# A transformer block on one core: LayerNorm's normalization moved to VectorE, and smaller changes of order, buffers and engines around it

## The chip, the cores and the metric

The kernel runs on one core of one Trainium2 chip. The time is device time in microseconds (us) of that core, as a median over executions. A ratio below is the mean time of one kernel's fast runs over that of the other's fast runs of the same rounds, on the same chip, so it is not quite the ratio of the medians that are quoted. "Faster" means faster by over 2% with a 95% interval.

Engines: TensorE (PE; PEld is its weight load), VectorE (DVE), ScalarE (ACT), GpSimd (POOL), and SyncE, which issues the DMAs.

## The reference

One pre-LayerNorm transformer block in bf16, with S = 2048 tokens, D = 1024, 32 heads of 32, and F = 3584:

```python
x = A_x
h = x + _A_ref(_layernorm(x, axis=-1), A_wqkv, A_wo)      # softmax(q k^T / sqrt(32)) v, then @ wo
h2 = h + _B_ref(_layernorm(h, axis=-1), B_w1, B_b1, B_w2, B_b2)   # gelu_tanh(. @ w1 + b1) @ w2 + b2
```

The exponentials of the softmax are the large fixed cost: 32 heads x 2048 x 2048. The kernel makes them on ScalarE in 1024 instructions of 128 x 1024 elements, which it calls `PT<-ps`: 967.2 us of busy time in the kernel before.

## The kernel before

The kernel builds a graph of tasks. A list scheduler with a cost model then fixes the order of each engine's instructions, and semaphores follow from the dependencies.

The stages, named by what ScalarE does:

- **Lead-in.** For each of four blocks of 512 tokens: LayerNorm, transposes, K and V (and, for the first block, Q) of head group 0, and then 8 exponentials for that block's keys: 32 in all. A head group is 4 heads; there are 8.
- **Middle.** Attention of four chunks of 512 queries. A chunk is 256 exponentials, 32 for each head group. In between, TensorE does background work on one PSUM bank: in chunk 0 the projections of the other groups (`rest_of_projections`), in chunks 1 to 3 the Q projections that were put off ("late Q"), and the output projection, LN2 and FFN of the chunk before.
- **Tail.** Output projection, LN2 and FFN of the last chunk, on eight PSUM banks, with no attention left.

LayerNorm: VectorE makes the statistics, GpSimd makes 1/sqrt with two `pow`, and one of the two subtracts and multiplies:

```python
def layer_norm(tiles, prio, norm="dve"):
    ...                                   # bn_stats, bn_aggr on VectorE; add, pow, pow on GpSimd
    for k, (x_ap, B_x, o_ap, B_o) in enumerate(tiles):
        eng, cost = (dve, 0.58) if norm == "dve" else (pool, 1.4)
        eng(lambda e, ...: e.tensor_scalar(o_ap, x_ap, mvr[...], rden[...], ALU.subtract, ALU.mult), cost, ...)

def x_slot(tt):                           # a ring of six tiles of x
    s = tt % 6
    ...
```

The lead-in and the projections after it:

```python
for tc in range(4):
    tts = list(range(4 * tc, 4 * tc + 4))
    ev = "act" if tc == 0 else "dve"      # who copies transposes out of PSUM
    for h in ((0, 1), (2, 3)) if tc == 0 else ((0, 1, 2, 3),):
        ln_tiles([tts[k] for k in h], 0, "dve" if tc == 0 else "pool")
        for k in h:
            tr_tile(tts[k], lb(), ev)
    ...
    proj(1, 0, tc, lb(), ev)              # K
    if tc == 0:
        proj(0, 0, 0, lb(), ev, direct=True)   # Q
    for k in range(8):
        att.qk(0, [(k % 2, 4 * tc + k // 2)])  # one unit: QK for one exponential
        ...                               # V after k == 1 and k == 3
        lead_pv(4)

def rest_of_projections():
    for g in range(1, G):
        for tc in range(4):
            proj(1, g, tc, 7, "dve")      # K, four token blocks
        proj(0, g, 0, 7, "dve")           # Q: to DRAM and back by DMA
        if g < 7:
            ...                           # V for a later group, four pieces
    for g in range(G):
        proj(0, g, 1, 7, "dve")           # Q of chunk 1, all groups
```

The end of a head group's attention, and the last stages:

```python
def finish(self, qc, g, pr, bank):
    dve(... Dsb <- ps ...); dve(... Osb <- ps ...)      # denominators, numerators
    if pr == 1:
        for k in range(4):
            dve(... v.reciprocal(Dsb[:, 128k:128k+128]) ..., 0.93)
        dve(... OT[:, g, :] = Osb * Dsb ...)            # one OT for all chunks

def wo_ln2(R, qc, banks):
    for j in range(2):                    # column half outer, row block inner
        for t4 in range(4):
            for k, g in enumerate([7, 0, 1, 2, 3, 4, 5, 6]):
                mm(bank, OT[:, g, t4 * P:(t4 + 1) * P], R.w1[:, s:s + 2, g, :], k == 0, k == 7, ...)
            ...
    for t4 in range(4):
        layer_norm(...); transposes(..., "dve", 0)

# ffn1: bias add, square, inner polynomial and product on VectorE, tanh on ScalarE
dve(... v.tensor_scalar(R.xh[:, i, :], psum[:, bank, :], b1f[:, fc:fc + 1], None, ALU.add) ...)

for qc in range(1, NCH):                  # the middle
    if qc + 1 < NCH:
        late_q(R1, qc + 1)
    wo_ln2(R1, qc - 1, [7])
    ffn1(R1, qc - 1, [7]); ffn2(R1, qc - 1, [7])
    attention_chunk(qc)
```

The softmax here doesn't subtract the row's maximum and nothing guards it: scores larger than these inputs give would overflow.

## Time and profile before

| | before |
|---|---|
| median of 3 runs | 1263.97 us (1263.61 to 1265.93) |
| span of the profiled run | 1261.5 us |
| lead-in, to the start of the 33rd exponential | 130.3 us |
| middle, to the end of the last exponential | 986.5 us |
| tail | 144.7 us |

The three stages are read from ScalarE's timeline: 1024 exponentials stand in it, so the 33rd start and the last end cut the span.

First the page of the kernel before: busy time by engine with its share of the span, then the busy tenths in 40 slices (PEclk is the clock granted to TensorE), then the chain of work that ended last, as shares of the span by engine. In what follows L638 is the exponential, L498 the normalization, L435 and L439 matmuls of projections and FFN, L649 and L653 the PV matmuls, L629 QK.

```profile
span 1261.5 us, 37733 instructions
PE 1154.2 (91%) x17266; PEld 465.2 (37%) x17276; DVE 686.6 (54%) x1186; ACT 1027.8 (81%) x1145; POOL 83.6 (7%) x108
...
ACT  3322899999999999999989999999999999940210
POOL 4760000000002000000010000000100000001000
PEclk8668999999899999999999999999999999978989
...
PE 57%; ACT 27%; DVE 10%; POOL 4%; issue 2%; DMA 0%; POOLq 0%; DVEq 0%
```

TensorE is busy for 91% of the span and ScalarE for 81%, so the average names no culprit. The slices do: ScalarE is nearly idle in the first four, where GpSimd has most of its work and the clock granted to TensorE sags, and again in the last five.

The groups of instructions, with shapes kept apart (count, busy us, mean ns of one; then the idle time before them and what ended it):

```profile
L638 ACT ACTIVATE PT<-ps 128x1024 bf16<-128x1024 f32 x1024 | 967.2, 1037 | 87.8 <-PE ps L629 79.6 <-PE ps L653 3.7
...
L498 POOL TENSOR_SCALAR xb<-xrb,mvr,rden 128x1024 bf16<-128x1024 bf16 x8 | 30.2, 3782 | 0.4 <-POOL rden L494 0.2 <-DVE st L483 0.2
...
L498 DVE TENSOR_SCALAR xb<-xrb,mvr,rden 128x1024 bf16<-128x1024 bf16 x2 | 1.0, 544 | 1.8 <-POOL rden L494 1.8
```

GpSimd needs 3782 ns for a 128 x 1024 tile that VectorE normalizes in 544 ns. Of ScalarE's 87.8 us of waiting before exponentials, nearly all is for QK (L629).

GpSimd's timeline in the lead-in (start, duration, engine, line, operation, count):

```profile
25.46 7.56 POOL L498 TENSOR_SCALAR xb<-xrb,mvr,rden 128x1024 bf16<-128x1024 bf16 x2 [0.19 <-POOL rden L494]
...
50.21 15.07 POOL L498 TENSOR_SCALAR xb<-xrb,mvr,rden 128x1024 bf16<-128x1024 bf16 x4 [0.18 <-DVE st L483]
...
73.91 7.55 POOL L498 TENSOR_SCALAR xb<-xra,mvr,rden 128x1024 bf16<-128x1024 bf16 x2
```

Three blocks of four tiles, 15.1 us each, start about 24 us apart (the first and the third are split into two rows of two tiles). So 15.1 us of a block's 24 are normalization on GpSimd. ScalarE's timeline at the end of the lead-in:

```profile
95.52 7.69 ACT L638 ACTIVATE PT<-ps 128x1024 bf16<-128x1024 f32 x8 [8.28 <-PE ps L629]
130.34 1.94 ACT L638 ACTIVATE PT<-ps 128x1024 bf16<-128x1024 f32 x2 [27.14 <-PE ps L629]
```

After 8 exponentials in 7.69 us, ScalarE waits 27.14 us for the first QK of head group 1. In that time TensorE makes that group's K (four blocks), Q and four V pieces.

The busy time of each engine by stage:

```profile
core 0: us, PE busy (x) PEld busy (x) DVE busy (x) ACT busy (x) POOL busy (x), PEclk, DMA share, GB/s
...
25.50:130.30 104.80, 74.33 (x1194) 37.26 (x1192) 41.55 (x87) 31.58 (x33) 50.13 (x20) 0.77 0.41 104
130.30:343.50 213.20, 208.31 (x3896) 92.71 (x3900) 105.19 (x213) 210.43 (x225) 0.00 (x0) 0.98 0.16 50
343.50:1116.80 773.30, 730.06 (x11396) 270.17 (x11388) 432.05 (x686) 761.10 (x853) 18.99 (x48) 0.99 0.32 94
...
1150.00:1206.30 56.30, 51.24 (x223) 22.62 (x226) 51.29 (x90) 13.24 (x21) 0.00 (x0) 0.95 0.33 93
```

In the lead-in no engine is near its limit, and the granted clock is 0.77. In the rest TensorE has 208.3 of 213.2 us in chunk 0 and ScalarE 210.4: both are nearly full. VectorE is nearly full (51.3 of 56.3 us) in the last row, which is the tail's FFN1; TensorE has as much (51.2), but its timeline shows that it is the one that waits:

```profile
1123.16 15.69 PE L439 MATMUL ps<-a_w1r,OT 128*128 128x512 bf16 x64 [5.69 <-issue]
...
1201.53 0.39 PE L439 MATMUL ps<-b2t,two_row 128*128 128x512 bf16 x1 [0.82 <-DVE b_xh L728]
1204.87 0.39 PE L439 MATMUL ps<-b2t,two_row 128*128 128x512 bf16 x1 [2.94 <-DVE b_xh L728]
1206.32 0.61 PE L439 MATMUL ps<-b2t,two_row 128*128 128x512 bf16 x1 [1.07 <-DVE b_xh L728]
1206.72 3.62 PE L439 MATMUL ps<-a_w2r,gT 128*128 128x512 bf16 x8
```

The output projection starts 6.4 us after the last exponential (1116.8). At the border to FFN2, TensorE waits for VectorE's bias adds (b_xh, L728), which hand back PSUM banks: the last FFN1 matmul ends at 1200.3, and the first FFN2 matmul with weights starts only at 1206.72. After that wait the granted clock is 0.50 (1206.7 to 1210.3): 8 matmuls take 3.62 us.

### The profile page before, as it was taken

To read this page: it belongs to the slowest core of one execution; us is meant where nothing else is said; L and a number is where in the kernel's file an instruction comes from. 1 tells how busy PE (TensorE), PEld (TensorE's weight loads), DVE (VectorE), ACT (ScalarE), POOL (GpSimd) and SP (SyncE) were. 2 spreads that over 40 slices of the span, in tenths; PEclk is the share of its full clock that TensorE was granted. 3 is DMA by queue.
4 is the path that set the end of the run, shared out by engine and by line. 5 is a ranking of instruction groups with operands and counts; after the bars stand their busy time and mean duration, and the time that the engine had idled before them with its cause. 6 is when DMAs were issued, how large, how long until landed. Compare 5 with 4: busy or idle time off the path is not lost.

```text
span 1261.5 us, 37733 instructions
## 1 busy us (share of the span) xinstructions
PE 1154.2 (91%) x17266; PEld 465.2 (37%) x17276; DVE 686.6 (54%) x1186; ACT 1027.8 (81%) x1145; POOL 83.6 (7%) x108
## 2 busy tenths in 40 slices
PE   6677999999999999999989999998899999977988
PEld 3333444443333333333333333332333333323434
DVE  5335355555347888223367884323688822337971
ACT  3322899999999999999989999999999999940210
POOL 4760000000002000000010000000100000001000
PEclk8668999999899999999999999999999999978989
DMA  5190020003333323144332331423333304402404
GB/s 134 53 250 30 15 82 15 15 17 121 101 105 90 94 85 111 35 123 144 112 104 61 93 94 35 135 65 117 98 110 103 101 18 124 130 17 59 117 12 139
DMA packets 163137, 109.26 MB, mean 87 GB/s; under 512 B 25377, under 2 KB 160417, under 8 KB 162466
## 3 DMA queue, kind: packets, MB, share of 16 engines
q1 hardware_dynamic: 162978, 106.85, 29.2%
q8 instruction: 135, 2.21, 0.7%
q14 instruction: 24, 0.20, 0.1%
HBM read 96.22 MB, written 10.35 MB: 84 GB/s over the span
## 4 chain that ended last, share of the span: by engine, by line
PE 57%; ACT 27%; DVE 10%; POOL 4%; issue 2%; DMA 0%; POOLq 0%; DVEq 0%
PE ps L435 30%; ACT PT L638 26%; PE ps L439 9%; PE ps L649 9%; PE ps L629 8%; POOL xb L498 4%; DVE a_xh L728 3%; DVE gT L736 1%; DVE stg L544 1%; DVE Dsb L667 1%; DVE a_uu L732 1%; PE ps L504 1%; DVE Osb L663 1%; DVE st L483 1%; DVE Dsb L661 1%
## 5 line engine op out<-in xcount | busy, mean ns | idle before, releaser
L638 ACT ACTIVATE PT<-ps 128x1024 bf16<-128x1024 f32 x1024 | 967.2, 1037 | 87.8 <-PE ps L629 79.6
L649 PE MATMUL ps<-PT,V 128*32 128x512 bf16 x2048 | 322.0, 392 | 8.3 <-DVE Osb L663 4.3
L653 PE MATMUL ps<-PT,ones_50 128*32 128x512 bf16 x2048 | 322.1, 392 | 0.0
L629 PE MATMUL ps<-QT_65,KT_63 32*128 32x512 bf16 x2048 | 211.1, 390 | 17.7 <-ACT PT L638 17.2
L435 PE MATMUL ps<-hnT,a_w1r 128*32 128x512 bf16 x3200 | 211.2, 382 | 14.9 <-DVE a_xh L728 13.9
L435 PE MATMUL ps<-a_w2r,gT 128*32 128x512 bf16 x2688 | 196.5, 381 | 0.0
L649 PEld LDWEIGHTS ps<-PT,V 128*32 128x32 bf16 x2048 | 96.8, 97 | 125.3 <-issue 36.0
L629 PEld LDWEIGHTS ps<-QT_65,KT_63 32*128 32x128 bf16 x2048 | 53.1, 91 | 222.4 <-ACT PT L638 173.5
L661 DVE COPY Dsb<-ps 64x512 f32<-64x512 f32 x64 | 44.4, 694 | 131.1 <-PE ps L653 129.8
L435 PE MATMUL ps<-xnT,Wall 128*32 128x512 bf16 x1536 | 107.4, 400 | 8.3 <-DVE stg L544 6.1
L435 PEld LDWEIGHTS ps<-hnT,a_w1r 128*32 128x32 bf16 x3200 | 72.6, 96 | 114.4 <-issue 38.5
L667 DVE RECIPROCAL Dsb<-Dsb 128x128 f32<-128x128 f32 x128 | 114.2, 926 | 1.0
L435 PEld LDWEIGHTS ps<-a_w2r,gT 128*32 128x32 bf16 x2688 | 68.5, 96 | 81.9 <-issue 28.3
L653 PEld LDWEIGHTS ps<-PT,ones_50 128*32 128x32 bf16 x2048 | 96.8, 97 | 0.0
L734 ACT ACTIVATE b_th<-b_uu 128x512 f32<-128x512 bf16 x28 | 17.6, 630 | 84.2 <-DVE b_uu L732 84.2
L728 DVE TENSOR_SCALAR a_xh<-ps,b1f 128x512 bf16<-128x512 f32 x84 | 63.0, 750 | 36.2 <-PE ps L435 34.4
L488 POOL CAST mvb<-mv 128x2 bf16<-128x2 f32 (+2 forms) x21 | 4.5, 218 | 1057.6 <-DVE mv L485 1057.6
L435 PE MATMUL ps<-Wall,xnT 128*32 128x256 bf16 x2048 | 67.3, 274 | 3.3 <-DVE V L602 2.4
L758 DVE SCALAR_TENSOR_TENSOR a_ost<-ps,hch 128x512 bf16<-128x512 f32 x24 | 16.4, 684 | 97.0 <-PE ps L435 96.9
L544 DVE CAST stg<-ps 128x512 bf16<-128x512 f32 x46 | 31.2, 678 | 55.7 <-PE ps L435 55.6
L435 PEld LDWEIGHTS ps<-xnT,Wall 128*32 128x32 bf16 x1536 | 37.4, 100 | 61.7 <-issue 20.6
L736 DVE SCALAR_TENSOR_TENSOR gT<-a_th,a_xh 128x512 bf16<-128x512 f32 x84 | 56.8, 676 | 3.3 <-ACT a_th L734 3.1
(65 smaller groups left out, 896.1 us busy)
## 6 DMA issues: line engine op xcount, KB each, us to landing
a_w2r<-in_B_w_dram SPq DMA_DIRECT2D x56, 512.0 KB, 5.5
a_w1r<-in_B_w_dram SPq DMA_DIRECT2D x42, 512.0 KB, 3.9
a_w1r<-in_A_wo_dram SPq DMA_DIRECT2D x16, 512.0 KB, 3.8
QT_65<-q_scratch SPq DMA_DIRECT2D x62, 128.0 KB, 2.8
b_w1r<-in_B_w_dram SPq DMA_DIRECT2D x14, 512.0 KB, 3.9
Wall<-in_A_wqkv_dram SPq DMA_DIRECT2D x16, 256.0 KB, 5.7
a_xr_81<-in_A_x_dram SPq DMA_DIRECT2D x32, 128.0 KB, 2.2
a_w1r<-in_A_wqkv_dram SPq DMA_DIRECT2D x8, 512.0 KB, 4.5
```

What stands on the lines that cost most here:

```text
L435: fns.append(lambda p, j=j: p.matmul(psum[32 * j:32 * j + 32, bank, c0:c1], lhsT[:, 32 * j:32 * j + 32], rhs, start=start, stop=stop, tile ...
L439: pe(lambda p: p.matmul(psum[:, bank, c0:c1], lhsT, rhs, start=start, stop=stop), occ, reads=reads, writes=[B_ps[bank]], mode="full")
L498: eng(lambda e, k=k, x_ap=x_ap, o_ap=o_ap: e.tensor_scalar(o_ap, x_ap, mvr[:, i + k, :], rden[:, i + k, :], ALU.subtract, ALU.mult), cost, ...
L544: dve(lambda v: v.tensor_copy(stg[:, s, :], psum[:, bank, :]), c_dve_ps(512), reads=[B_ps[bank]], writes=[B_stg[s]])
L629: return p.matmul(psum[:, 2 * u + j, :], KT2[r0:r0 + 32, p16, tc, i, :], QT2[r0:r0 + 32, qs, pr, :], start=True, stop=True, tile_position= ...
L638: act(lambda a, u=u, s=s: a.activation(PT[:, s, :, :], psum[:, 2 * u:2 * u + 2, :], ACT.Exp, bias=0.0, scale=SCALE), 1024, reads=[B_ps[2 * ...
L649: fns.append(lambda p, j=j, h=h: p.matmul(psum[32 * j:32 * j + 32, bank, :], V[:, kt, 32 * h:32 * h + 32], PT[:, s, j, :], start=first, st ...
L653: fns.append(lambda p, j=j: p.matmul(psum[64 + 32 * j:96 + 32 * j, bank, :], ones32[:, :], PT[:, s, j, :], start=first, stop=last, tile_po ...
L661: dve(lambda v: v.tensor_copy(Dsb[64 * pr:64 * pr + 64, :], psum[64:128, bank, :]), c_dve_ps(512), reads=[B_ps[bank]], writes=B_Dsb[pr], p ...
L667: dve(lambda v, k=k: v.reciprocal(Dsb[:, 128 * k:128 * k + 128], Dsb[:, 128 * k:128 * k + 128]), 0.93, reads=[B_Dsb[0][k], B_Dsb[1][k]], w ...
L728: dve(lambda v, i=i, fc=fc, bank=bank: v.tensor_scalar(R.xh[:, i, :], psum[:, bank, :], b1f[:, fc:fc + 1], None, ALU.add), c_dve_ps(512), ...
L736: dve(lambda v, i=i, fc=fc: v.scalar_tensor_tensor(gT[:, fc, :], R.th[:, i, :], 1.0, R.xh[:, i, :], ALU.add, ALU.mult), c_dve(512), reads= ...
```

## The change

The intent: take the normalization off GpSimd in the lead-in, close the hole before head group 1, let the attention output of a chunk be written while that of the chunk before is still being read, use LN2's waits for late Q, and unload VectorE in the last FFN. The core of the diff, cut where marked:

```diff
-    def schedule(self, pick_pe, switch=0.1, dma_rate=190.0, ...):
+    def schedule(self, pick_pe, switch=0.1, dma_rate=280.0, ...):      # scheduler's own cost model
-    OT, B_OT = sb(top, "OT", [P, G, 512], BF, G)
-    xrb, B_xrb = sb(ot_lo, "xrb", [P, 4, D], BF, 4)
+    OT, B_OT_ = sb(top, "OT", [P, 2, G, 512], BF, 2 * G, 4)            # one per parity of the chunk
+    xrb, B_xrb = sb(ot_lo, "xrb", [P, 8, D], BF, 8)                    # x ring of 8 instead of 6
...
-    for k in range(20):
-        pe(lambda p: p.matmul(psum[:, 7, :], ident[:, :], b2t[:, 0:512], ...), 0.44, ... prio=-9)
+    for k in range(80):
+        pe(lambda p: p.matmul(psum[:, 6, 0:256], ident[:, :], b2t[:, 0:256], ...), 0.12, ... kind="warm")
...
     for tc in range(4):
-            ln_tiles([tts[k] for k in h], 0, "dve" if tc == 0 else "pool")
+            ln_tiles([tts[k] for k in h], 0, "dve")
             for k in h:
-                tr_tile(tts[k], lb(), ev)
+                tr_tile(tts[k], lb(), "act")
...
-        for k in range(8):
-            att.qk(0, [(k % 2, 4 * tc + k // 2)])
+        for k in range(4):
+            att.qk(0, [(k % 2, 4 * tc + k // 2), (1 - k % 2, 4 * tc + 2 + k // 2)])
...
     def rest_of_projections():
         for g in range(1, G):
+            proj(0, g, 0, 7, "dve", direct=(g == 1))      # direct: copied by VectorE, no DRAM
             for tc in range(4):
                 proj(1, g, tc, 7, "dve")
-            proj(0, g, 0, 7, "dve")
...
-        for g in range(G):
+        for g in range(2):
             proj(0, g, 1, 7, "dve")
...
-        if qc + 1 < NCH:
-            late_q(R1, qc + 1)
-        wo_ln2(R1, qc - 1, [7])
+        if qc == 1:
+            late_q(R1, 1, 2)
+        wo(R1, qc - 1, [7], R1)
+        ln2(R1, qc - 1, [7], (lambda qc=qc: late_q(R1, qc + 1, 0)) if qc + 1 < NCH else None)   # inside LN2
...
-        for j in range(2):
-            for t4 in range(4):
-                for k, g in enumerate([7, 0, 1, 2, 3, 4, 5, 6]):
+        for t4 in range(4):
+            for j in range(2):
+                for k, g in enumerate([7, 0, 1, 2, 3, 4, 5, 6] if len(banks) == 1 else range(G)):
...
-                dve(lambda v, ...: v.tensor_scalar(R.xh[:, i, :], psum[:, bank, :], b1f[:, fc:fc + 1], None, ALU.add), ...)
+                if len(banks) == 1:
+                    dve(... as before ...)
+                else:                                                   # the tail
+                    act(lambda a, ...: a.activation(R.xh[:, i, :], psum[:, bank, :], ACT.Identity,
+                                                    bias=b1f[:, fc:fc + 1], scale=1.0), ...)
```

Also: the last head group's attention output is written in four pieces of 128 columns; the tail's transposes are copied out by ScalarE; late Q reads its own buffer instead of LN2's; the tail gets more buffers for x (8 instead of 2) and for normalized tiles (4 instead of 2); GpSimd's costs in the scheduler's model are raised to what they are; and TensorE's chooser prefers PV once no QK is left.

## The prediction

> **What bounds it now** (span 1261.5 us). ScalarE's timeline gives three stages.
> - Lead-in, 0 to 130.3 us: only 32 of 1024 exponentials. The chain of waits shows GpSimd normalizing three token blocks, 15.1 us each (3782 ns a tile in the groups table; VectorE needs 540 ns). Then ScalarE idles 27.1 us: K, Q and V of the second head group are all projected before its first QK.
> - Middle, 130.3 to 1116.8 us: ScalarE-bound. Back-to-back exponentials start every 0.92 us, a tanh adds 0.53: 992 x 0.92 + 84 x 0.53 = 957 us of 987. TensorE is nearly full too (29 to 31 of each 31.5 us in the stage table), so the chain wanders between both.
> - Tail, 1116.8 to 1261.5 us: output projection, LN2, last FFN. 520 matmuls at 0.215 us need 112 us. TensorE waits about 6 us for the last reciprocals, 11 us in LN2, 6.4 us for VectorE (51 busy us in 56, GELU).
>
> **What the change does**
> 1. Twelve normalizations go to VectorE: 45 us of GpSimd becomes 6.5 us. [...] this trace says seven times slower than VectorE. ScalarE takes all 16 transpose evictions. Per block ScalarE has 12 x 0.92 = 11.1 us, VectorE about 10.8, TensorE about 10: a period of 12 us instead of 24.
> 2. Warm-up matmuls, and the first Q copied by VectorE instead of four DMAs (2.5 us): first exponential at 22.4 instead of 25.5 us. ([...] in the trace matmuls start every 0.43 us at 16 to 20 us, 0.21 when warm.) 61 warm-up matmuls stand before the first transposes and may delay those by 1 to 2 us.
> 3. Next head group: Q first, QK as soon as one K block is there: the 27 us hole nearly closes. Lead-in ends near 70 us: 60 us saved.
> 4. Middle: same exponentials and tanhs, so ScalarE's floor stands. TensorE loses its 27 us head start; six Q projections (1.7 us each) move from chunk 0 to chunk 1; late Q fills LN2's waits; double-buffered attention output frees the output projection. TensorE needs about 907 us of 960 (estimate: counts x 0.216 us, 0.2 us of mode switches per QK). Stalls stay about 30 us. No gain: 989 us.
> 5. Tail: output projection and LN2 overlap by row block (-4.5 us, 13 matmuls run early); bias on ScalarE leaves VectorE 28 x 1.6 = 45 us, below TensorE's 48, so the 6.4 us wait and a cold start go (-8). 132 instead of 144.7 us.
>
> Sum: 70 + 989 + 132 = 1191 us of span, 1193 us of device time.
>
> **Prediction: 1193 us, 8 in 10 between 1176 and 1212.** Faster by over 2%: 0.97; within 2%: 0.02; slower: 0.01.
>
> **What would show it.** Right: the 33rd exponential starts at 66 to 76 us; no ScalarE gap over 5 us after it; GpSimd busy about 40 us; exponential spacing in chunk 0 0.94 to 0.97 us; last exponential to end 128 to 136 us; no TensorE gap over 2 us before FFN2. Wrong: lead-in blocks over 15 us apart, or chunk 0 at 1.0 us or more per exponential (TensorE-bound, late K or V).
>
> **What would make it wrong.** VectorE's in-order queue in the lead-in, where statistics stand before K copies; TensorE unable to feed chunk 0 without its head start (10 to 20 us lost); or the LN2 changes removing more middle stalls than I allow (10 us gained).

Two clauses that no trace of this case shows are cut from it. No term of its sum is among them: 70 + 989 + 132 = 1191 us stands as recorded. Three things that it names are seen in traces as follows. The "mode switches" are steps at which the tile shape of the matmuls changes: in the kernel before, the step from a projection (128*32, at 99.44 us) to a QK (32*128, at 99.76) is 0.32 us and the one back (to 100.08) is 0.32, against 0.22 with no change (to 100.30), so 0.2 us for each QK. The "cold start" is the stretch at a granted clock of 0.50 after the wait before FFN2. And that VectorE keeps the order of its queue is seen in e2, below: copies whose PV matmuls had started at 613.50 ran at 626.65, behind the product of 625.25, though VectorE sat idle for 0.39 us in between (before 618.55).

## The result, and the profile after

| | before | changed |
|---|---|---|
| median, first comparison (4 runs each) | 1264.24 us (1263.61 to 1265.93) | 1202.87 us (1199.85 to 1419.73) |
| ratio of the fast runs | | 0.9505 (0.9484 to 0.9525): faster |
| lead-in, to the 33rd exponential | 130.3 | 75.4 |
| middle | 986.5 | 995.5 |
| tail | 144.7 | 129.3 |
| span | 1261.5 | 1200.2 |

One of the four runs of the changed kernel was slow: 1419.7 us at a mean granted clock of 0.749, against 0.99 in the other three. It happened to be the profiled one. Its profile is left aside. None of the runs in the experiments below was slow, this kernel's four included, and why that one was stays open. The profile of the changed kernel shown here is that of the first experiment, which runs it unedited.

The stages sum as 1261.5 - 1200.2 = 61.3 = 54.9 (lead-in) - 9.0 (middle) + 15.4 (tail). The lead-in gave most of it, the tail a quarter, and the middle took some back.

The page of the changed kernel. L643 is now the exponential, L439 and L443 are the matmuls that were L435 and L439, and L654 and L634 are PV and QK (L658 is the other half of PV, for the denominators):

```profile
span 1200.2 us, 37857 instructions
PE 1129.4 (94%) x17336; PEld 464.4 (39%) x17336; DVE 668.6 (56%) x1165; ACT 1059.8 (88%) x1189; POOL 38.2 (3%) x96
...
ACT  4889898979999999999999999999999999963620
POOL 2100000000110000000200000000100000002000
PEclk9999999999999999999999999999999999987999
...
PE 73%; ACT 13%; DVE 11%; issue 1%; DMA 1%; POOL 1%; SPq 0%; POOLq 0%; DVEq 0%
```

GpSimd is down from 83.6 to 38.2 us, the clock no longer sags in the first slices, and the chain that ended last has moved from ScalarE (27% to 13%) to TensorE (57% to 73%).

Groups by form:

```profile
L643 ACT ACTIVATE PT<-ps 128x1024 bf16<-128x1024 f32 x1024 | 967.2, 1034 | 30.2 <-PE ps L634 17.4 <-PE ps L658 9.3
...
L502 DVE TENSOR_SCALAR xb<-xrb,mvr,rden 128x1024 bf16<-128x1024 bf16 x16 | 7.9, 538 | 2.7 <-POOL rden L498 2.6
```

All 16 lead-in tiles are normalized at 538 ns. ScalarE's idle time before exponentials fell from 87.8 to 30.2 us. ScalarE's timeline, in four places:

```profile
32.38 1.94 ACT L643 ACTIVATE PT<-ps 128x1024 bf16<-128x1024 f32 x2 [0.56 <-PE ps L634]
...
72.72 1.94 ACT L643 ACTIVATE PT<-ps 128x1024 bf16<-128x1024 f32 x2 [0.78 <-PE ps L634]
75.44 5.61 ACT L643 ACTIVATE PT<-ps 128x1024 bf16<-128x1024 f32 x6 [0.78 <-PE ps L634]
...
124.57 1.02 ACT L643 ACTIVATE PT<-ps 128x1024 bf16<-128x1024 f32 x1 [1.08 <-PE ps L658]
127.52 2.86 ACT L643 ACTIVATE PT<-ps 128x1024 bf16<-128x1024 f32 x3 [1.92 <-PE ps L658]
...
269.10 1.02 ACT L643 ACTIVATE PT<-ps 128x1024 bf16<-128x1024 f32 x1 [3.26 <-PE ps L634]
```

Four things are to be seen. In the lead-in ScalarE waits 0.56 us or more after nearly every second exponential. The 27 us hole is gone: 72.72 to 75.44 is the border to head group 1. And in chunk 0 there are now waits of 1.08 and 1.92 us, this time for PV (L658); the kernel before had one long wait for PV, of 3.56 us, and that at a chunk's border and not in chunk 0. The last line is a wait of another kind, 3.26 us for the first QK of head group 7; TensorE's timeline puts that QK (268.65) behind the DMA that brings Q. The busy time by stage, with the columns of the table shown for the kernel before:

```profile
23.90:75.40 51.50, 45.34 (x920) 25.41 (x916) 27.68 (x69) 42.17 (x45) 4.94 (x8) 1.00 0.69 186
75.40:299.90 224.50, 212.31 (x4116) 98.00 (x4120) 114.34 (x235) 210.11 (x224) 0.00 (x0) 1.00 0.15 47
299.90:1070.90 771.00, 734.56 (x11506) 272.67 (x11506) 438.02 (x690) 762.64 (x853) 18.55 (x48) 0.99 0.34 100
...
1095.70:1146.80 51.10, 51.05 (x225) 22.64 (x226) 44.40 (x79) 32.08 (x54) 0.00 (x0) 0.95 0.36 103
```

The first of these rows is the lead-in, now at a clock of 1.00. The second is chunk 0 after the lead-in: the same 224 exponentials take 224.5 instead of 213.2 us, at the same ScalarE busy time. In FFN1 (last row) VectorE has fallen from 51.3 to 44.4 us and TensorE is full (51.05 of 51.1). TensorE in the tail:

```profile
1072.08 11.18 PE L443 MATMUL ps<-a_w1r,OT 128*128 128x512 bf16 x51
...
1146.60 0.38 PE L443 MATMUL ps<-b2t,two_row 128*128 128x512 bf16 x1
1146.81 3.40 PE L443 MATMUL ps<-a_w2r,gT 128*128 128x512 bf16 x15
```

Of the 64 output-projection matmuls, 13 have already run by 1072.08, 1.2 us after the last exponential. FFN2 follows FFN1 without a wait: its first matmul, for the bias, starts at 1146.60, and the first with weights at 1146.81; at a clock of 1.00, 15 of them take 3.40 us.

### The profile page after: what moved, and what is told of

Same layout as the page of the kernel before. It is cut to its first block, busy times and chain, and to the rows that moved or that the text cites. A ratio compares the mean times of both kernels' runs of the same rounds, so it can differ in the third digit from the quotient of the medians.

```text
span 1417.9 us, 37847 instructions
## 1 busy us (share of the span) xinstructions
PE 1366.2 (96%) x17326; PEld 510.9 (36%) x17336; DVE 673.2 (47%) x1165; ACT 1085.3 (77%) x1189; POOL 37.9 (3%) x96
## 4 chain that ended last, share of the span: by engine, by line
PE 91%; ACT 4%; DVE 3%; issue 1%; POOL 1%; DMA 0%; POOLq 0%; DVEq 0%
PE ps L439 48%; PE ps L654 17%; PE ps L634 12%; PE ps L443 10%; ACT PT L643 3%; PE ps L658 2%; PE ps L798 1%; ACT xnT L512 1%; DVE a_xh L748 1%; PE ps L508 1%; DVE V L606 0%; DVE stg L547 0%; DVE Osb L668 0%; DVE Dsb L666 0%; DMA a_w1r<-in_A_wqkv_dram 0%
## 5 line engine op out<-in xcount | busy, mean ns | idle before, releaser
L643 ACT ACTIVATE PT<-ps 128x1024 bf16<-128x1024 f32 x1024 | 989.2, 1025 | 180.5 <-PE ps L634 166.1
L654 PE MATMUL ps<-PT,V 128*32 128x512 bf16 x2048 | 383.4, 457 | 13.7 <-DVE V L606 6.2
L658 PE MATMUL ps<-PT,ones 128*32 128x512 bf16 x2048 | 384.8, 458 | 0.0
L439 PE MATMUL ps<-a_w2r,gT 128*32 128x512 bf16 x2688 | 241.9, 452 | 0.0
L634 PE MATMUL ps<-QT,KT 32*128 32x512 bf16 x2048 | 216.7, 414 | 7.4 <-ACT PT L643 7.3
L439 PE MATMUL ps<-a_hnT,a_w1r 128*32 128x512 bf16 x2688 | 215.2, 454 | 4.0 <-DVE a_xh L748 3.2
L654 PEld LDWEIGHTS ps<-PT,V 128*32 128x32 bf16 x2048 | 103.3, 104 | 143.9 <-issue 89.3
L634 PEld LDWEIGHTS ps<-QT,KT 32*128 32x128 bf16 x2048 | 51.5, 91 | 272.3 <-ACT PT L643 164.5
L439 PE MATMUL ps<-xnT,Wall 128*32 128x512 bf16 x1344 | 111.6, 453 | 7.0 <-ACT xnT L512 4.8
L439 PEld LDWEIGHTS ps<-a_w2r,gT 128*32 128x32 bf16 x2688 | 77.3, 109 | 112.0 <-issue 103.3
L439 PEld LDWEIGHTS ps<-a_hnT,a_w1r 128*32 128x32 bf16 x2688 | 70.6, 107 | 108.0 <-issue 71.4
L658 PEld LDWEIGHTS ps<-PT,ones 128*32 128x32 bf16 x2048 | 103.5, 104 | 6.6 <-issue 6.6
L666 DVE COPY Dsb<-ps 64x512 f32<-64x512 f32 x64 | 44.4, 694 | 101.5 <-PE ps L658 100.1
L439 PE MATMUL ps<-Wall,xnT 128*32 128x256 bf16 x2048 | 83.8, 314 | 0.0
L443 PE MATMUL ps<-a_hnT,b_w1r 128*128 128x512 bf16 x219 | 64.5, 470 | 2.1 <-ACT a_hnT L512 1.5
L439 PEld LDWEIGHTS ps<-Wall,xnT 128*32 128x32 bf16 x2048 | 57.6, 107 | 22.7 <-issue 11.3
L443 PE MATMUL ps<-a_w2r,gT 128*128 128x512 bf16 x219 | 64.1, 461 | 0.5
L439 PE MATMUL ps<-a_w1r,OT 128*32 128x512 bf16 x768 | 63.1, 453 | 0.8 <-DVE hch L719 0.5
```

What stands on the lines that cost most here:

```text
L439: fns.append(lambda p, j=j: p.matmul(psum[32 * j:32 * j + 32, bank, c0:c1], lhsT[:, 32 * j:32 * j + 32], rhs, start=start, stop=stop, tile ...
L443: pe(lambda p: p.matmul(psum[:, bank, c0:c1], lhsT, rhs, start=start, stop=stop), occ, reads=reads, writes=[B_ps[bank]], mode="full")
L634: return p.matmul(psum[:, 2 * u + j, :], KT2[r0:r0 + 32, p16, tc, i, :], QT2[r0:r0 + 32, qs, pr, :], start=True, stop=True, tile_position= ...
L643: act(lambda a, u=u, s=s: a.activation(PT[:, s, :, :], psum[:, 2 * u:2 * u + 2, :], ACT.Exp, bias=0.0, scale=SCALE), 1024, reads=[B_ps[2 * ...
L654: fns.append(lambda p, j=j, h=h: p.matmul(psum[32 * j:32 * j + 32, bank, :], V[:, kt, 32 * h:32 * h + 32], PT[:, s, j, :], start=first, st ...
L658: fns.append(lambda p, j=j: p.matmul(psum[64 + 32 * j:96 + 32 * j, bank, :], ones32[:, :], PT[:, s, j, :], start=first, stop=last, tile_po ...
```

## The experiments

All twelve kernels gave correct results. The kernel before ran on the same chips in the same rounds: 1264.43 us on the chip of the first four, 1265.05 on that of the next four, 1264.95 on that of the last four. Ratios are to it. Two measures come from each trace. The *33rd* is the start of the 33rd exponential. A *stall* of a stretch is its duration less 0.9217 us for each exponential and 0.53 us for each tanh (in the trace of the kernel before, the median step from one exponential to the next is 0.921 us, and from a tanh to an exponential 0.52).

| run | kernel | median us | ratio (95%) | 33rd | middle | tail |
|---|---|---|---|---|---|---|
| e1 | changed, unedited | 1202.05 | 0.9503 (0.9479-0.9526) | 75.4 | 995.5 | 129.3 |
| e2 | before + normalization on VectorE | 1240.57 | 0.9812 (0.9795-0.9828) | 95.7 | 996.7 | 144.3 |
| e3 | changed, normalization back on GpSimd | 1225.51 | 0.9691 (0.9663-0.9718) | 94.8 | 996.3 | 128.5 |
| e4 | changed, tail's bias back on VectorE | 1210.32 | 0.9571 (0.9557-0.9585) | 75.2 | 998.1 | 136.5 |
| e5 | changed, one-unit QK in the lead-in | 1211.48 | 0.9577 (0.9563-0.9592) | 80.1 | 1000.2 | 129.0 |
| e6 | changed, Q after K again | 1211.80 | 0.9575 (0.9548-0.9601) | 89.7 | 994.1 | 129.0 |
| e7 | changed + a group of chunk 1 brought forward | 1190.73 | 0.9412 (0.9398-0.9426) | 75.0 | 985.0 | 128.8 |
| e8 | before + x ring of 8 | 1255.83 | 0.9915 (0.9890-0.9939) | 113.4 | 995.8 | 144.8 |
| e9 | changed, single attention output | 1203.64 | 0.9524 (0.9511-0.9537) | 75.2 | 997.8 | 128.4 |
| e10 | changed, late Q before the output projection | 1202.09 | 0.9504 (0.9491-0.9518) | 74.1 | 995.4 | 128.6 |
| e11 | e7 with fewer warm-up matmuls | 1189.54 | 0.9408 (0.9394-0.9422) | 73.5 | 985.0 | 127.5 |
| e12 | changed, output projection in column order | 1203.38 | 0.9514 (0.9501-0.9527) | 75.0 | 996.7 | 129.8 |

### e1: the changed kernel again

No edit.

> The changed kernel once more, unedited, because its first profile fell in a run of 1419.7 us at a granted clock of 0.749, while its other three runs took 1200 to 1203 us at 0.99. If the slow run was a state of the chip, the fast runs here are again 1200 to 1205 us at 0.99 and a fast profile shows the stages: 33rd exponential at 66 to 76 us, middle near 989 us, tail near 132 us by my prediction; one of the three must be some 10 us longer, and I guess the middle (TensorE without its head start) or the lead-in. If the change itself brings the lower clock on, several of these runs are slow.

Measured: 1202.05 us (1198.0 to 1205.24). The stages stand above. The slow run did not come back.

### e2: the normalization alone

```diff
 # in before
-            ln_tiles([tts[k] for k in h], 0, "dve" if tc == 0 else "pool")
+            ln_tiles([tts[k] for k in h], 0, "dve")
```

> The kernel before with one edit: the twelve GpSimd normalizations of the lead-in on VectorE. My theory: each of three blocks shortens from 24 us to about 14 us, since VectorE still has the transpose evictions: about 1236 us, 28 us less than before. Rival: the blocks are held by other waits (one QK unit at a time, evictions), and the gain is under 15 us.

The lead-in shrank by 34.6 us (130.3 to 95.7): exponentials of successive blocks now begin 12.0 to 13.8 us apart. But the time fell only by 24, against 28 expected. The middle grew by 10.2 us. Most of that lies at one place: exponentials 512 to 576, the first of chunk 2, have a stall of 16.5 us, against 6.2 in the kernel before. ScalarE's timeline there:

```profile
628.77 2.85 ACT L638 ACTIVATE PT<-ps 128x1024 bf16<-128x1024 f32 x3 [11.34 <-PE ps L653]
```

And VectorE's:

```profile
601.08 2.57 DVE L667 RECIPROCAL Dsb<-Dsb 128x128 f32<-128x128 f32 x3
...
625.25 0.64 DVE L669 TENSOR_TENSOR OT<-Osb,Dsb 128x512 bf16<-128x512 f32 x1
...
626.65 0.69 DVE L661 COPY Dsb<-ps 64x512 f32<-64x512 f32 x1
```

The chain reads: the reciprocals of a head group are done at 603.65, but the product into OT (L669) runs only at 625.25, after the output projection has read the old chunk's OT and after LN2's statistics, which VectorE's queue put before it. Only then does VectorE copy the next group's denominators and numerators out (626.65 to 628.04; the last PV matmuls before the gap had started at 613.50), which frees the PV bank (the profile names a small VectorE copy just behind, ending at 628.10, as what PV waited for; the chain is a reading of the timelines); PV resumes at 628.10 and ScalarE, after 11.34 us, at 628.77. The kernel before has the same chain with a smaller gap (3.56 us at 655.64). So a gain in the lead-in opened a wait half the kernel away, presumably because the order of the background work moves with it; no run holds that order fixed.

### e3: everything but the normalization

```diff
 # in the changed kernel
-            ln_tiles([tts[k] for k in h], 0, "dve")
+            ln_tiles([tts[k] for k in h], 0, "dve" if tc == 0 else "pool")
```

> The changed kernel with the twelve normalizations back on GpSimd. If the normalization is the larger part of the lead-in gain, about 30 us is lost: 1233 us. If two-unit QK and ScalarE evictions carry the gain, under 15 us is lost.

Undoing the move costs 23.5 us in the median (1225.51 - 1202.05), between the two amounts expected. The profiled run was the fastest of the four (1221.42 us): its span is 19.4 us longer than e1's, and all of that is the lead-in, which loses less than the 34.6 us that e2 gained. In its trace GpSimd's blocks start at 21.62, 39.55 and 57.49, so every 18 us and not every 24. With eight x tiles the statistics of the next block are made while GpSimd still normalizes; the ring had been part of the 24 us. e8 tests that reading.

### e4: the bias

```diff
 # in the changed kernel, ffn1
-                if len(banks) == 1:
+                if True:
```

> The changed kernel with the bias of the last FFN back on VectorE. My theory: VectorE is again the longer engine of that GELU (28 x 2.3 us against TensorE's 48 us), a gap of about 6 us before FFN2 returns, and one cold start: 1209 to 1211 us, 6 to 8 us more. Rival: the gap before was due to something else, and under 3 us is lost.

The tail grows from 129.3 to 136.5 us and the time by 8.3 us. TensorE's waits before FFN2 come back (1.01, 2.87 and 0.85 us); the longest is:

```profile
1153.51 0.61 PE L443 MATMUL ps<-b2t,two_row 128*128 128x512 bf16 x1 [2.87 <-DVE b_xh L748]
```

FFN2 again starts slowly: its first 7 matmuls with weights take 3.19 us from 1155.36, where the changed kernel had 15 in 3.40 us. The bias is worth 7 to 8 us, as predicted.

### e5: one QK unit at a time in the lead-in

```diff
-        for k in range(4):
-            att.qk(0, [(k % 2, 4 * tc + k // 2), (1 - k % 2, 4 * tc + 2 + k // 2)])
-            if k < 2:
-                proj_v(4 * tc + 2 * k, 0, lb(), ev)
+        for k in range(8):
+            att.qk(0, [(k % 2, 4 * tc + k // 2)])
+            if k in (1, 3):
+                proj_v(4 * tc + k - 1, 0, lb(), ev)
             lead_pv(4)
```

> The changed kernel with the lead-in's QK back to one unit at a time. In the changed kernel's lead-in ScalarE waits 0.56 to 0.66 us for QK after every second exponential (12 of 16 pairs in its timeline). My theory: with only two units of PSUM, a QK for both has to wait until both exponentials are read, so two-unit QK serializes; one unit at a time lets one QK run under the other's exponential, and up to 16 x 0.6 = 9 us of the lead-in goes: 33rd exponential at 67 to 72 us instead of 75.4, 1195 to 1199 us. Rival: TensorE and its mode switches limit the lead-in, the 16 more QK issues (about 0.4 us each) cost 3 to 6 us: 1205 to 1208 us.

The lead-in's blocks take 13.0 to 14.2 us instead of the predicted 12, and the waits of 0.56 us after each pair looked like the cause: the kernel has only two PSUM units there, and a QK that fills both can start only when both are free. On that theory one unit at a time should be faster. The theory fell. ScalarE's timeline:

```profile
36.24 7.62 ACT L643 ACTIVATE PT<-ps 128x1024 bf16<-128x1024 f32 x8 [1.16 <-PE ps L634]
...
51.05 5.64 ACT L643 ACTIVATE PT<-ps 128x1024 bf16<-128x1024 f32 x6 [3.53 <-PE ps L634]
...
80.12 1.94 ACT L643 ACTIVATE PT<-ps 128x1024 bf16<-128x1024 f32 x2 [7.46 <-PE ps L634]
```

The small waits are indeed gone: 8 exponentials run back to back in 7.62 us. But then ScalarE waits 3.53, 2.61 (at 64.97) and 7.46 us at the block borders for the first QK of the next block, which needs that block's K. The waits had only been gathered at the border. The 33rd starts 4.7 us later, the middle is 4.7 us longer, and the time is 9.4 us longer. So two-unit QK is worth about 9 us, more than the rival allowed. Whether it gains by fewer QK issues on TensorE or by the order the scheduler finds around it was not isolated; and since both variants have blocks of 13 to 15 us, it seems to be TensorE's path to the next K that sets the block's period, not the pairing.

### e6: Q after K again

```diff
         for g in range(1, G):
-            proj(0, g, 0, 7, "dve", direct=(g == 1))
             for tc in range(4):
                 proj(1, g, tc, 7, "dve")
+            proj(0, g, 0, 7, "dve")
```

> The changed kernel with the second head group's Q last again, after its four K blocks, and through the scratch tensor in HBM. If Q first closed the 27 us hole, a ScalarE gap of 15 to 25 us returns after the 32nd exponential; the head start it gives TensorE should take away the stalls of 3.5, 3.6 and 6.8 us in chunk 0 (net 10 to 17 us more: 1212 to 1219 us). Rival: the hole came from the scheduler's assumed DMA rate (190 against 280), which this run leaves at 280; then the gap stays under 8 us and the time within 3 us of the changed kernel's.

With `direct` gone, the Q of group 1 takes the way through DRAM again (`load_q` follows). ScalarE's timeline at the border to head group 1, and TensorE's behind it:

```profile
73.66 1.94 ACT L643 ACTIVATE PT<-ps 128x1024 bf16<-128x1024 f32 x2 [0.78 <-PE ps L634]
89.69 1.94 ACT L643 ACTIVATE PT<-ps 128x1024 bf16<-128x1024 f32 x2 [14.09 <-PE ps L634]
```

```profile
89.25 0.40 PE L634 MATMUL ps<-QT,KT 32*128 32x512 bf16 x4 [1.43 <-DMA QT<-q_scratch]
```

A hole of 14.09 us is back: QK waits at last for the DMA that brings Q, after K and V pieces have gone ahead of it. It costs 9.8 us of time. So this part, the order and the way by DRAM together, closes about half of the kernel before's 27 us hole, and the rival that it was the scheduler's new DMA rate alone, with a small hole expected here, is out. The other 13 us of the old hole come from the rest of the change, that rate included (in the kernel before, QK stood behind all four V pieces); which part is not isolated.

The expectation also said that this head start would take the stalls of chunk 0 away. Two of three went (1.5, 1.0 and 8.3 us, against 3.5, 3.6 and 6.8), and with them all of chunk 0's waits for PV. The third is now one wait of 7.14 us at 281.36 for the first QK of head group 7, whose matmuls stand behind late Q's: those wait 2.76 us for a DMA of their weights.

### e7: give TensorE its head start back

Before head group 1 of chunk 0, the group-0 attention of chunk 1 is run: its K and V exist already, so only one more Q projection is needed for 32 exponentials. TensorE meanwhile projects ahead. The total work is the same. Slot 2 of the Q ring is used for it.

```diff
     def rest_of_projections():
+        proj(0, 0, 1, 7, "dve", direct=True)       # Q of chunk 1, group 0, into slot 2
         for g in range(1, G):
...
-        for g in range(2):
-            proj(0, g, 1, 7, "dve")
+        proj(0, 1, 1, 7, "dve")
...
     rest_of_projections()
+    attention_chunk(1, last=2)
     attention_chunk(0, first=2)
...
-        attention_chunk(qc)
+        attention_chunk(qc, first=2 if qc == 1 else 0)
```

> The changed kernel with one change of order: after the lead-in, attention of chunk 1's first head group (its K and V are there, only one more Q is needed) runs before chunk 0's second. My theory: the chunk-0 stalls at the even head groups (exponentials 64 to 96, 128 to 160, 192 to 224: 3.5, 3.6, 6.8 us) are projections of V that come late since TensorE has no head start; 29 us of exponentials that need no new projections give it 14 us of head start. Stalls there fall to about 1 us each: 8 to 11 us less, 1191 to 1194 us. Rival: the stalls come from hand-offs of the one projection bank or from evictions on VectorE; they stay, and the time is that of the changed kernel within 3 us.

The middle falls from 995.5 to 985.0 us and the time to 1190.73 us, 0.941 of the kernel before. The stalls, stretch by stretch (e7 runs one head group of chunk 1 first, so its even groups of chunk 0 are one column further right):

| exponentials | 64-96 | 96-128 | 128-160 | 160-192 | 192-224 | 224-256 | sum 32-256 |
|---|---|---|---|---|---|---|---|
| before | 0.9 | 1.0 | 0.9 | 0.8 | 0.9 | 1.0 | 6.7 |
| changed (e1) | 3.5 | 1.2 | 3.6 | 1.0 | 6.8 | 1.3 | 18.1 |
| e7 | 0.8 | 0.8 | 1.2 | 1.5 | 0.6 | 1.6 | 7.2 |

The even groups have 0.8, 1.5 and 1.6 us where the changed kernel had 3.5, 3.6 and 6.8; chunk 0's last group, beyond the table, has 0.3.

Where the changed kernel had its waits of 1.08 and 1.92 us, e7's ScalarE runs 124 exponentials in one piece:

```profile
74.96 117.60 ACT L643 ACTIVATE PT<-ps 128x1024 bf16<-128x1024 f32 x124 [0.78 <-PE ps L634]
```

In chunk 0 of the changed kernel ScalarE waited 9.0 us for PV in six waits, and TensorE 5.3 us for VectorE's copies of V; e7 has no such wait of ScalarE in its list. Its 3.26 us for head group 7's QK are gone too; that wait was for Q by DMA, not for V. V arrives late every second group, since a V projection serves two; in the kernel before, the 27 us hole had let TensorE make V ahead. The theory that chunk 0 is short of TensorE's head start holds, and e6, where a hole gave a head start in another way, agrees for the waits for V.

### e8: the x ring alone

```diff
 # in before
-        s = tt % 6
-        return (xra[:, s, :], B_xra[s]) if s < 2 else (xrb[:, s - 2, :], B_xrb[s - 2])
+        s = tt % 8
+        return (xra[:, s, :], B_xra[s]) if s < 4 else (xrb[:, s - 4, :], B_xrb[s - 4])
```

The buffer and the prefetch (`tt + 8`) are enlarged to match.

> The kernel before with one edit: eight token tiles in flight instead of six, normalization still on GpSimd. In the changed kernel with GpSimd normalization, blocks started every 18 us, GpSimd working without a break; in the kernel before they start every 24.2 us with about 9 us between. My theory: before, the next block's statistics wait for tiles that can be loaded only after the block is normalized, so the ring of six is worth up to 6 us a block: 33rd exponential at 112 to 118 us instead of 130, about 1250 us. Rival: the break comes from the serial chain on VectorE and TensorE after the normalization; under 5 us gained.

GpSimd's timeline shows the blocks 18 us apart (the first starts at 25.95):

```profile
43.83 15.08 POOL L498 TENSOR_SCALAR xb<-xra,mvr,rden 128x1024 bf16<-128x1024 bf16 x4
...
61.67 15.07 POOL L498 TENSOR_SCALAR xb<-xrb,mvr,rden 128x1024 bf16<-128x1024 bf16 x4
```

The 33rd moves from 130.3 to 113.4. But the time falls by only 9 us (to 1255.83, where about 1250 was expected), since the middle grows by 9.3: the stall at exponentials 512 to 576 rises from 6.2 to 13.6 us, as in e2. So the ring was worth 17 us of the old lead-in, and the reading of e3 is confirmed. (With the normalization on VectorE its worth was not tested, so the gains of e2 and e8 can't be added.)

### e9 and e10: the attention output and late Q

e9 writes every chunk's output into one OT again (`OT[:, 0, ...]` and its buffers instead of `qc % 2`). e10 puts late Q in front of the output projection again:

```diff
+        if qc + 1 < NCH:
+            late_q(R1, qc + 1, 0)
         wo(R1, qc - 1, [7], R1)
-        ln2(R1, qc - 1, [7], (lambda qc=qc: late_q(R1, qc + 1, 0)) if qc + 1 < NCH else None)
+        ln2(R1, qc - 1, [7])
```

> The changed kernel with the attention output in one buffer again (the memory stays). In the runs that shorten only the lead-in (e2, e8) ScalarE stalls 16.5 and 13.6 us between exponentials 512 and 576, 6.2 us in the kernel before: the product that writes the first head group's output of the next chunk waits for the output projection of the last chunk, VectorE's queue stands behind it, the value accumulation's bank is not emptied and no exponential finds a free buffer. My theory: the second buffer is what removes this, so 4 to 16 us of stall come back at one or more chunk starts (exponentials 256 to 320, 512 to 576, 768 to 832): 1206 to 1216 us. Rival: the output projection now comes ahead of the late Q and is done in time, so one buffer is enough: within 3 us of 1202.

> The changed kernel with the late Q of the next chunk before the output projection, as in the kernel before, not inside LN2. My theory: with two output buffers ScalarE does not wait for TensorE's work there, TensorE has slack by the end of each chunk, so within 3 us of 1202. Rival: filling LN2's waits is worth something: 3 to 10 us more, with stalls of ScalarE at exponentials 256 to 384 and 512 to 640.

e9 has 1203.64 us and e10 1202.09 us; against e1's ratio of 0.9503 they have 0.9524 and 0.9504, with intervals that overlap it. The stall at 512 to 576 is 1.5 us in e1, 1.4 in e9 and 3.1 in e10, against 6.2 in the kernel before, 13.6 in e8 and 16.5 in e2. So the theory of e9 missed, and that of e10 held. Undoing either part alone doesn't bring the stall back, so either one suffices to keep it away, if one of them is what removed it. Both undone together in the changed kernel was not run, so that "if" stays open.

### e11: fewer warm-up matmuls

```diff
 # in e7; the scheduler believes a warm-up to be longer, and places 43 instead of 61 before the transposes end
-        pe(lambda p: p.matmul(psum[:, 6, 0:256], ident[:, :], b2t[:, 0:256], ...), 0.12,
+        pe(lambda p: p.matmul(psum[:, 6, 0:256], ident[:, :], b2t[:, 0:256], ...), 0.17,
```

> The version of e7 (1190.7 us) with fewer warm-up matmuls ahead of the first transposes (43 instead of 61; the rest stand behind them). In the changed kernel the 61 end at 12.4 us, while the first two normalized tiles are there at about 10 us. 43 should end near 9.8 us: first exponential 1.5 to 2.5 us earlier than 23.9 us, 1188 to 1190 us. Rival: the second pair of tiles or the weights set the pace there, and nothing is gained (1190 to 1192).

The first transposes start at 9.77 us instead of 11.90, and the first exponential at 22.6 instead of 23.7 (both against e7). The time is 1189.54 us (1187.79 to 1191.94), 1.2 us below e7, with overlapping intervals: inconclusive in time, though the trace shows the delay. It is the fastest version, 0.9408 of the kernel before.

### e12: the output projection in column order

```diff
-        for t4 in range(4):
-            for j in range(2):
+        for j in range(2):
+            for t4 in range(4):
```

> The changed kernel with its output projection column half by column half again, not row block by row block. By my account the row order lets LN2 start under the output projection: the tail (last exponential to end) is 129 us, and should grow by 3 to 6 us, to 1205 to 1208 us, with the FFN's first matmul at 28 to 31 us after the last exponential instead of 24.8. Rival: LN2 starts after the projection either way (TensorE waits 5.9 us between the two in the changed kernel), and under 2 us is lost; then the tail's gain came from the early matmuls and from ScalarE's share of the evictions.

1203.38 us, with a ratio whose interval overlaps that of e1: the expected 3 to 6 us did not come. FFN1 starts 25.2 us after the last exponential, against 24.8. So the row-block order, to which the prediction gave the gain, does next to nothing.

## Why the prediction was right or wrong

The total was right: 1193 us predicted, 1202.87 measured, inside 1176 to 1212. In span the sum of stages was 70 + 989 + 132 = 1191; measured 75.4 + 995.5 + 129.3 = 1200.2. Two errors of +5.4 and +6.5 us added, and one of -2.7 took a little away. That last one is luck: the tail came near its number by another way than the predicted one, as step 5 below shows.

- **Step 1, normalization and the period of the lead-in: mechanism right, size off.** The move rested on the trace of the kernel before: 3782 ns a tile on GpSimd against 542 to 544 ns on VectorE (538 in e1). e2 and e3 show the move to be worth 24 and 23.5 us. The mis-sized term is "a period of 12 us instead of 24": it was 13.0 to 14.2 for the first three blocks, because ScalarE cannot run its 11.1 us of work without waiting for TensorE's next K and QK. e5 shows that the pairing of QK is not to blame. Also, part of the old 24 us was the x ring of six, which the step did not name: e8 gives it 17 us alone.
- **Step 2, warm-up and direct Q: half of its size.** The first exponential came at 23.9 us, not 22.4 (25.5 before). The delay of 1 to 2 us by the warm-ups was foreseen but not put into the sum: 61 of them end at 12.35 us, and e11 gets 1.1 us of it back. In the trace of the kernel before, matmuls of 512 columns start 0.43 us apart at 16 to 20 us, where the granted clock is 0.50, and 0.21 to 0.216 us apart later. The mean clock of the old lead-in was 0.77, that of the new one 1.00. No run takes the warm-up matmuls out (e11 only moves 18 of them behind the transposes), so what they do for the clock was not shown.
- **Step 3, Q first: right.** The hole closed to 0.8 us; e6 reopens 14.1 us of it. The rest of the closing was not isolated. The four blocks took 51.5 us against the 47.6 of the sum (70 - 22.4); with 1.5 us of a later first exponential, that makes up the 5.4 us.
- **Step 4, the middle: this step failed.** It said "Stalls stay about 30 us", "No gain: 989 us". The middle took 995.5 us, 9 more than before. Chunk 0 has 11.4 us more of stalls (18.1 against 6.7), the border at 512 to 576 has 4.7 fewer (1.5 against 6.2), and 2.3 us lie elsewhere. The step itself named the lost head start of 27 us and yet gave it no cost in the sum; it appeared only among the things that might make the prediction wrong, as "TensorE unable to feed chunk 0 without its head start (10 to 20 us lost)". That is what happened, and e7 shows it by giving a head start back: the stalls of exponentials 32 to 256 fall to 7.2 us. Of the changed kernel's waits there, 9.0 us were for PV behind a late V and 3.26 us for a Q that came late by DMA; both are gone in e7, and the 9.0 in e6 as well. The average, 907 of 960 us of TensorE work, hid that V projections, and once a Q, are due at fixed times in chunk 0. The sign the prediction set for being wrong, 1.0 us or more for an exponential in chunk 0, is there: 224.5 / 224 = 1.002.
- **Step 4, late Q and the double-buffered output: no gain, as predicted, for the changed kernel (e9, e10).** What e2 and e8 add is that without these parts, a shorter lead-in opens a stall of 13 to 17 us at the border; which part of the change prevents it stays open.
- **Step 5, the tail: size nearly right, one mechanism wrong.** Predicted 132, measured 129.3. The bias gave 7.2 us in e4 against 8 predicted: both the 6.4 us of waits before FFN2 and the start at a clock of 0.50 after them are gone (it is 1.00 in e1). "Output projection and LN2 overlap by row block (-4.5 us, ...)" was wrong as to the mechanism, though 13 matmuls do run early: LN2 waits as long as before, 12.5 us from the end of the output projection to FFN1 against 11.2, and e12 shows the order to be worth nothing clear. The gain, 8.4 us to FFN1's start, came from the output projection itself, which ended 12.3 us after the last exponential instead of 22.0. Its matmuls no longer begin with head group 7, whose attention output comes last and now arrives in pieces of 128 columns. That this is the cause is argued from the trace; no run took it alone, nor the tail's larger x buffers.

## What to carry to other kernels

Idle time at the start of a pipeline may be paying for something: before closing such a hole, list the work that the idle engine's partner does in it, and ask by when the next stage needs that work; an average over the stage won't show it. Here the remedy was not to reopen the hole but to fill it with work whose inputs already exist (e7, where the lead-in stays as short and the middle loses 10.5 us). When a static scheduler orders everything, a local gain can open a wait far away (e2, e8), so compare the stages, not only the total. And when small waits follow every step, take them away in an experiment before believing they cost anything: in e5 they only moved to the border and grew.

## What the traces measured of the engines

- A 128 x 1024 bf16 `tensor_scalar` with two per-partition operands took 3782 ns on GpSimd and 535 to 544 ns on VectorE (kernel before and e1), a factor of 7. Successive tiles on GpSimd start as far apart as that (four in 15.07 us), so it is not an artefact of the profiler's spans.
- A 128-partition `pow` on GpSimd took 557 to 583 ns for one column and 1007 to 1057 ns for four (kernel before and e1). By the difference within each of the two instructions that is roughly 150 to 170 ns for each further column, an estimate (the profile's own notes call spans on GpSimd rough).
- One run of this one-core program, out of four in the first comparison, had a mean granted clock of 0.749 with TensorE 96% busy, and took 1419.7 us. No run here shows what limited it, or what the other cores of the chip were doing.
- After a VectorE `tensor_scalar` of that shape that took 550 ns, the next instruction started 460 ns after its start (614.88 to 615.34 in e2).
- In the trace of the kernel before, the step from a QK to the next matmul, which has another tile shape (32*128, then 128*32), is 0.32 to 0.33 us, against 0.216 us between matmuls of one shape: about 0.1 us for each change. In e1 the step from a PV matmul (128*32) to one of the output projection (128*128) is 0.33 us as well (1071.75 to 1072.08).
